# The product of gate and up: runs of seven columns and a strided write, in place of strided reads and a plain write

## The chip, the cores and the metric

The kernel runs on one core of a Trainium2 chip. The metric is device time in microseconds (us) from one execution of the whole kernel; several executions are run, and their median is compared.

A core has five engines with queues of their own: PE (matrix multiply, with weight loads shown as PEld), DVE (VectorE), ACT (ScalarE), POOL (GpSimd) and SP, which here only issues transfers. Sixteen DMA engines move data between the chip's main memory and SBUF, the on-chip memory of 128 partitions. PE writes to PSUM, a second on-chip memory of 128 partitions and eight banks of 512 fp32 columns. Engines wait for each other through semaphores.

## The reference, cut to what matters

One token passes through an attention layer with a long cache and a gated feed-forward layer, both with a layer norm in front and a residual.

```python
x = A_x                                            # (1, 1, 512) bf16
h = x + _A_ref(_layernorm(x), A_k_cache, A_v_cache, A_wq, A_wo)
h2 = h + _B_ref(_layernorm(h), B_w_gate, B_w_up, B_w_down)

def _A_ref(x, k_cache, v_cache, wq, wo):           # 32 query heads, 8 key heads, 65536 keys of 128
    q = x @ wq; scores = q . k * 128 ** -0.5
    return softmax(scores) . v @ wo

def _B_ref(x, w_gate, w_up, w_down):               # 512 -> 1792 -> 512
    g = x @ w_gate; u = x @ w_up
    return (sigmoid(g) * u) @ w_down
```

The caches of keys and values are 128 MiB each, so most of the work is reading 282 MB. What the change touches is `sigmoid(g) * u`, 1792 products.

## The kernel before, in words

There is no planner: every operation is recorded in program order on the queue of one engine by a helper (`op`, and `dma` for transfers), with the names of the operations that it depends on. From these the helper makes the waits. Each queue then runs strictly in that order.

The body walks through eight key heads. SP issues the loads of each head's keys and values in pieces. DVE transposes the keys in 256 blocks (line 531), PE multiplies them with the queries, DVE and ACT make the softmax, and PE multiplies with the values. When the last head is through, PE applies `wo`, and the tail of the kernel follows, one step behind the other:

- `ln_stats` and `ln_rstd` (lines 400 to 414) make the layer norm of `h`; line 834 writes the centred column `hc`.
- Lines 842 to 851: PE multiplies `hc` with the weights of gate, then with those of up. Each result is split over four partitions (0, 32, 64 and 96), 448 columns each, in PSUM banks `GB` and `UB`. Column `14 q + r` of partition `32 c` is element `448 c + 14 q + r` of the 1792, with `q` from 0 to 31 and `r` from 0 to 13.
- Line 854: ACT makes `tanh` of gate; line 855: DVE turns it into the scaled gate `sg2` (fp32, SBUF). Both come before the last matmul of up, which waits for the last weights of up.
- Lines 857 to 863, on DVE, in two halves `i` of seven values of `r` each (`HH`): a product (line 859) multiplies up, read from PSUM, with `sg2`, and writes `hh` (bf16, SBUF) in the order `32 r + q`; a transpose of 32 by 32 blocks (line 863) then turns each block `r` of `hh` into a column of `hhT` with the elements `q` on the partitions. The order on DVE's queue is product 0, transpose 0, product 1, transpose 1. Product 0 waits for the last matmul of up (`gu1`) and for `sg2`; each transpose waits for its product.
- Lines 871 to 882: PE multiplies each of the 14 columns of `hhT` with its rows of `w_down`, in four matmuls a column, so 56 in all. The first waits for transpose 0, the 29th for transpose 1; four loads of `w_down` (`wd0` to `wd3`) are waited for on the way.
- Lines 884 to 886: DVE and ACT copy the sum out of PSUM, and SP stores it.

The instructions run on all 128 partitions, of which four hold values. The tiles: `hh` is 128 by 448 bf16, `hhT` 128 by 480 bf16; the half of a product is 224 elements per partition. The profile writes `sg` for `sg` and `sg2`, and `PS` for all of PSUM.

Some other lines whose rows the prediction uses: 391 and 392 are reductions on DVE over the same 128 by 128 fp32 tile (391 reads every fourth column, 392 the columns in order); 634 is a product that lays out the attention's output; 410 to 412 are layer norm steps on one column; 566 is a reduction of PSUM columns in runs of eight. Line 432 writes four bf16 values per partition, 16 elements apart. Line 500 copies 64 bf16 values per partition on ACT, from runs of 16 to places eight elements apart (`NC` is 8):

```python
dst = bass.AP(tensor=ktw, offset=W0 + NC - 1, ap=[[KTW_ROW, 128], [WJ, 4], [NC, 16]])
src = bass.AP(tensor=qz, offset=64 * h, ap=[[512, 128], [16, 4], [1, 16]])
```

Of the kernel before, what the change touches and what calls it, by code (L numbers as in the profile page):

```python
# [10 lines left out]
ALU = mybir.AluOpType  # L11
# [24 lines left out]
class Prog:  # L36
# [14 lines left out]
    def op(self, eng, fn, deps=(), name=None, to=None, times=1):  # L51
        assert name is None or name not in self.where, name
        self.ops[eng].append(dict(fn=fn, deps=[d for d in deps if d], name=name, dma=None, to=to, times=times, part=self.part.get(eng)))
        if name:
            self.where[name] = (eng, len(self.ops[eng]) - 1)
# [168 lines left out]
def bass_sequential_preLN__gqa_block_cached__glu_gated_glu__decode_kernel(  # L224
# [15 lines left out]
    NF = FF // 128  # L240
# [4 lines left out]
    FG = FF // 4  # L245

    with ExitStack() as es:
        def sb(name, shape, dt):
            return es.enter_context(nc.sbuf_tensor(name, shape, dt))
# [51 lines left out]
        sg2 = sb("sg2", [128, FG], fp32)  # L301
        hh = sb("hh", [128, FG], bf16)
# [12 lines left out]
        def ps(bank, c0, c1, p0=0, p1=128):  # L315
            return PS[p0:p1, bank * 512 + c0: bank * 512 + c1]
# [311 lines left out]
        YT, STB, GB, UB, YB, OT = 0, MISC, 2, 3, 5, (1, 1)  # L628
# [228 lines left out]
        HH = ((0, 7), (7, NF))  # L857
        for i, (r0, r1) in enumerate(HH):
            op("dve", lambda e, r0=r0, r1=r1: e.tensor_tensor(  # L859
                hh[:, 32 * r0:32 * r1].rearrange("p (r q) -> p r q", q=32),  # L860
                ps(UB, 0, FG).rearrange("p (q r) -> p r q", r=NF)[:, r0:r1, :],
                sg2[:, :].rearrange("p (q r) -> p r q", r=NF)[:, r0:r1, :], ALU.mult), ["gu1", "sg2"], f"hh{i}")
            op("dve", lambda e, r0=r0, r1=r1: e.transpose(hhT[:, 32 + 32 * r0:32 + 32 * r1], hh[:, 32 * r0:32 * r1]), [f"hh{i}"], f"hhT{i}")  # L863
        def down(e, out_, lhsT, rhs, g, end):

# [51 lines left out]
```

## Time and profile before

| | |
|---|---|
| runs: median (lowest to highest) | 656.91 us (656.45 to 657.18) |
| span of the profiled execution, first to last instruction | 655.0 us |
| PE busy | 397.5 us (61%) |
| DVE busy | 350.3 us (53%) |
| ACT busy | 43.1 us (7%) |
| moved by DMA | 282.33 MB, mean 431 GB/s |
| mean granted clock of PE | 0.786 |

For the profiled execution the page gives the span alone; against the median of the runs, 1.9 us lie around it.

How to read the rows. A group row has the line, the engine, the operation, what is written and read with its shape and type, the count, and then busy us, mean ns of one | idle us of the engine before them, and what ended it. A timeline row has the start and the length in us ahead of that. A row by stretches has the stretch, its length, then the busy time (and count) of PE, PEld, DVE, ACT and POOL, the granted clock of PE as a share of full speed, the busy share of the DMA engines, and GB/s; where it was asked of one line alone, only that line's engines stand in it. The chain that ended last is followed back from the last instruction: each step is what released the next one. "Issue" is time in which an engine waited for nothing that the profile shows.

### The profile page before, as it was taken

What the parts mean: (1) busy time and instruction counts of PE and PEld (TensorE: products, weight loads), DVE (VectorE), ACT (ScalarE), POOL (GpSimd) and SP (SyncE); (2) the same over time, 40 slices, a digit from 0 to 9 for tenths busy, and PEclk for the clock granted to TensorE, in tenths of its full rate; (3) what the DMA queues carried; (4) which work ended last, traced back from release to release, by engine and by line L of the source; (5) the groups of instructions that cost most, each with busy time, mean ns of one, the idle gap of its engine ahead of it and who ended that gap; (6) DMA issues with size and microseconds to landing.
All of it is one profiled execution on the core that took longest, in us unless ns stands there. A gap on an engine that the chain in (4) does not pass through costs nothing.

```text
span 655.0 us, 6176 instructions
## 1 busy us (share of the span) xinstructions
PE 397.5 (61%) x2317; PEld 66.7 (10%) x1549; DVE 350.3 (53%) x428; ACT 43.1 (7%) x114; POOL 3.7 (1%) x19
## 2 busy tenths in 40 slices
PE   2778672937548293674828467392845739285466
PEld 1100010110101000010100101010010101001122
DVE  3398853819266290935719184481917548092202
ACT  1100200020000200002000200002000020001101
POOL 1000000000000000000000000000000000000000
PEclk9799695977959687785968769596796958878656
DMA  9999999999999999999999999999999989999998
GB/s 400 432 434 462 424 408 448 448 448 412 420 448 448 432 400 448 448 448 404 428 448 448 436 396 448 448 448 416 416 448 448 448 384 448 448 448 424 417 412 363
DMA packets 6372, 282.33 MB, mean 431 GB/s; under 512 B 738, under 2 KB 868, under 8 KB 1252
## 3 DMA queue, kind: packets, MB, share of 16 engines
q1 hardware_dynamic: 6340, 282.33, 99.7%
q10 hardware_dynamic: 32, 0.00, 0.0%
HBM read 282.33 MB, written 0.00 MB: 431 GB/s over the span
## 4 chain that ended last, share of the span: by engine, by line
DMA 66%; DVE 30%; PE 2%; issue 1%; SPq 0%; PEldq 0%
DMA ring<-in_A_k_cache_dram 58%; DVE ktw L531 30%; DMA ring<-in_B_w_up_dram 4%; DMA ring<-in_A_v_cache_dram 4%; PE PS L443 2%; PE PS L866 0%; PE PS L847 0%; DVE hh L859 0%; DVE hhT L863 0%; SPq L368 0%; SPq L339 0%; DVE y_sb L884 0%; PEldq L171 0%
## 5 line engine op out<-in xcount | busy, mean ns | idle before, releaser
L531 DVE STREAM_TRANSPOSE ktw<-ring 128x1024 f32<-128x1024 f32 x256 | 291.5, 1208 | 165.0 <-DMA ring<-in_A_k_cache_dram 165.0
L443 PE MATMUL PS<-ktw 128*128 128x512 bf16 x1024 | 276.3, 419 | 163.4 <-DVE ktw L531 155.8
L443 PE MATMUL PS<-ring,PT_sb 128*32 x1024 | 85.0, 420 | 55.0 <-issue 46.6
L443 PEld LDWEIGHTS PS<-ktw 128*128 x256 | 26.2, 102 | 401.5 <-issue 234.3
L618 ACT ACTIVATE po_sb<-PS,rl 128x512 bf16<-128x512 f32 x8 | 5.5, 687 | 523.4 <-PE PS L443 523.4
L443 PEld LDWEIGHTS PS<-ring,PT_sb 128*32 x1024 | 20.7, 116 | 117.5 <-issue 116.2
L566 DVE TENSOR_REDUCE gmj<-PS 1x4 f32<-1x128 f32 x8 | 2.2, 278 | 53.5 <-PE PS L564 53.5
L538 DVE TENSOR_REDUCE M_sb<-PS 128x1 f32<-128x512 f32 x32 | 19.9, 683 | 19.3 <-PE PS L443 19.3
L577 ACT ACTIVATE P_sb<-PS,negmax 128x512 bf16<-128x512 f32 x32 | 21.6, 686 | 0.3
L587 DVE STREAM_TRANSPOSE PT_sb<-P_sb 128x512 bf16<-128x512 bf16 x32 | 19.9, 674 | 1.7 <-ACT P_sb L577 1.7
L443 PE MATMUL PS<-ktw,xz 128*8 x32 | 9.6, 476 | 6.1 <-DMA ktw<-in_A_wq_dram 6.1
L634 DVE TENSOR_TENSOR Lw<-O,blk_of 128x896 bf16<-128x896 bf16 (+1 forms) x2 | 1.4, 682 | 15.9 <-ACT O L624 15.9
L489 DVE STREAM_TRANSPOSE qt<-qh 32x512 bf16<-32x512 bf16 x1 | 0.7, 699 | 14.8 <-ACT qh L486 14.8
L571 PE MATMUL PS<-one_f,gmrep 1*128 1x1 f32 x16 | 4.7, 358 | 5.0 <-DVE gmrep L568 5.0
L564 PE MATMUL PS<-identf,gm 128*1 128x128 f32 x16 | 4.5, 380 | 5.1 <-issue 2.9
L643 DVE CAST O<-PS 128x28 bf16<-128x28 f32 (+1 forms) x2 | 0.3, 174 | 12.8 <-PE PS L640 12.8
L577 ACT ACTIVATION_READ_ACCUMULATOR P_sb<-PS,negmax 128x1 f32 x32 | 6.5, 203 | 0.0
L621 PE MATMUL PS<-sel_bf,po_sb 128*128 128x4 bf16 x32 | 2.1, 170 | 6.3 <-ACT po_sb L618 6.3
L504 ACT ACTIVATE PS<-zcol 128x512 f32<-128x512 bf16 x8 | 5.0, 622 | 0.0
L573 ACT ACTIVATE negmax<-PS 128x1 f32<-128x1 f32 x8 | 1.4, 171 | 54.0 <-PE PS L571 54.0
L571 PEld LDWEIGHTS PS<-one_f,gmrep 1*128 1x128 f32 x16 | 4.0, 307 | 8.8 <-DVE gmrep L568 8.8
L592 PE MATMUL PS<-L_sb,lsel 128*128 128x4 f32 x16 | 2.5, 229 | 3.8 <-DVE PT_sb L587 3.8
(90 smaller groups left out, 65.4 us busy)
## 6 DMA issues: line engine op xcount, KB each, us to landing
ring<-in_A_k_cache_dram SPq DMA_DIRECT2D x4, 4096.0 KB, 34.8
ring<-in_A_v_cache_dram SPq DMA_DIRECT2D x1, 5120.0 KB, 30.1
ktw<-in_A_wq_dram SPq DMA_DIRECT2D x1, 4096.0 KB, 12.2
ktw<-in_A_wo_dram SPq DMA_DIRECT2D x1, 3584.0 KB, 18.4
ring<-in_A_v_cache_dram SPq DMA_DIRECT2D x1, 3072.0 KB, 36.9
ring<-in_B_w_gate_dram SPq DMA_DIRECT2D x1, 1792.0 KB, 23.4
ring<-in_B_w_up_dram SPq DMA_DIRECT2D x1, 1792.0 KB, 27.2
ring<-in_B_w_down_dram SPq DMA_DIRECT2D x1, 1024.0 KB, 29.2
```

The source lines that it names most:

```text
L443: return e.add_instruction(mybir.InstMatmult(name=nc.get_next_instruction_name(), engine=mybir.EngineType.PE, ins=[rhs, lhsT], outs=[e.low ...
L504: op("act", lambda e: e.activation(ps(PO, 0, 512), bass.AP(tensor=zcol, offset=0, ap=[[1, 128], [0, 512]]), AF.Copy), ["zcol"] if h == 0 e ...
L531: op("dve", lambda e, d=dst, sr=src: e.transpose(d, sr), deps, f"T{b}.{c}", to="T")
L538: op("dve", lambda e, u=u: e.tensor_reduce(M_sb[:, u % 4:u % 4 + 1], ps(u % NS, 0, 512), AX.X, ALU.max), [f"S{b}.{NC - NR + k}"], f"mx{u}" ...
L564: op("pe", lambda e: e.matmul(ps(MISC, 0, 128, 0, 1), lhsT=gm[:, :], rhs=identf[:, :], start=True, stop=True), [f"gm{h}"], f"gmT{h}", to="Q")
L566: op("dve", lambda e: e.tensor_reduce(gmj[:, :], ps(MISC, 0, 128, 0, 1).rearrange("p (i a c) -> p a i c", a=4, c=NC), AX.XY, ALU.max), [f" ...
L571: op("pe", lambda e: e.matmul(ps(MISC, 128, 129), lhsT=gmrep[0:1, :], rhs=one_f[0:1, 0:1], start=True, stop=True), [f"gmrep{h}"], f"neg{h}")
L577: op("act", lambda e, b=b: e.activation(P_sb[:, (b % 4) * 512:(b % 4 + 1) * 512], ps(b % NS, 0, 512), AF.Exp, bias=negmax[:, k:k + 1], sca ...
L587: op("dve", lambda e, b=b: e.transpose(PT_sb[:, (b % 4) * 512:(b % 4 + 1) * 512], P_sb[:, (b % 4) * 512:(b % 4 + 1) * 512]), [f"E{b}"], f" ...
L592: op("pe", lambda e: e.matmul(ps(MISC, 132, 136), lhsT=lsel[:, :], rhs=L_sb[:, :], start=True, stop=True), [f"PT{NR * h + NR - 1}"], f"l{h ...
L618: op("act", lambda e: e.activation(po_sb[:, :], ps(PO, 0, 512), AF.Copy, scale=rl[:, :]), [f"PV{h}.{NR - 1}", f"rl{h}"], f"po{h}", to="po")
L621: op("pe", lambda e, t=t: e.matmul(ps(OX, 0, 4), lhsT=po_sb[:, t * 128:(t + 1) * 128], rhs=sel_bf[:, 8 * t:8 * t + 8:2], start=(t == 0), s ...
```

## The change

Both products of line 859 walk their three operands in another order. Before, the outer loop is over `r` and the inner one over `q`: the reads of up (PSUM) and `sg2` (SBUF) step by 14 fp32 elements, 56 bytes, and the write to `hh` is plain. After, the outer loop is over `q` and the inner one over `r`: the reads go in runs of seven neighbouring fp32 elements, and the write to `hh` steps by 32 bf16 elements, 64 bytes. Each element ends where it did before, and the transposes and all else stay.

```diff
         HH = ((0, 7), (7, NF))
         for i, (r0, r1) in enumerate(HH):
             op("dve", lambda e, r0=r0, r1=r1: e.tensor_tensor(
-                hh[:, 32 * r0:32 * r1].rearrange("p (r q) -> p r q", q=32),
-                ps(UB, 0, FG).rearrange("p (q r) -> p r q", r=NF)[:, r0:r1, :],
-                sg2[:, :].rearrange("p (q r) -> p r q", r=NF)[:, r0:r1, :], ALU.mult), ["gu1", "sg2"], f"hh{i}")
+                hh[:, 32 * r0:32 * r1].rearrange("p (r q) -> p q r", q=32),
+                ps(UB, 0, FG).rearrange("p (q r) -> p q r", r=NF)[:, :, r0:r1],
+                sg2[:, :].rearrange("p (q r) -> p q r", r=NF)[:, :, r0:r1], ALU.mult), ["gu1", "sg2"], f"hh{i}")
             op("dve", lambda e, r0=r0, r1=r1: e.transpose(hhT[:, 32 + 32 * r0:32 + 32 * r1], hh[:, 32 * r0:32 * r1]), [f"hh{i}"], f"hhT{i}")
```

## The prediction

> **What bounds the kernel now.** I read the page first: the span, the line on DMA, and the shares of the chain that ended last.
>
> ```profile
> span 655.0 us, 6176 instructions
> ...
> DMA  9999999999999999999999999999999989999998
> ...
> DMA 66%; DVE 30%; PE 2%; issue 1%; SPq 0%; PEldq 0%
> ```
>
> The 16 DMA engines are busy in every slice: over most of the span the kernel runs at the pace of its loads, with VectorE's transposes next. The change lies in the last five microseconds, so its worth has to be read there. Next came the chain in order of time, cut to its end (start, length, what).
>
> ```profile
> 621.60 27.22 DMA ring<-in_B_w_up_dram
> 648.82 0.04 issue
> 648.86 1.69 PE PS L847 x16
> 650.55 0.02 issue
> 650.58 0.54 DVE hh L859
> 651.12 0.02 issue
> 651.14 0.42 DVE hhT L863
> 651.57 0.14 issue
> 651.70 1.79 PE PS L866 x50
> 653.49 0.03 issue
> 653.51 0.28 DVE y_sb L884
> ```
>
> The last block of weights of up lands at 648.82, its matmuls end at 650.55, and from there every step waits for the one before it. The first product (L859) is on that chain itself. The timeline of the same stretch gives both products, both transposes and the matmuls behind them.
>
> ```profile
> 650.58 0.53 DVE L859 TENSOR_TENSOR hh<-PS,sg 128x224 bf16<-128x224 f32 x1 [1.15 <-PE PS L847]
> 651.14 0.41 DVE L863 STREAM_TRANSPOSE hhT<-hh 128x224 bf16<-128x224 bf16 x1
> 651.48 0.49 DVE L859 TENSOR_TENSOR hh<-PS,sg 128x224 bf16<-128x224 f32 x1
> 651.67 1.43 PEld L866 LDWEIGHTS PS<-ring,hhT 128*32 128x32 bf16 x52 [0.71 <-DMA ring<-in_B_w_down_dram]
> 651.70 1.77 PE L866 MATMUL PS<-ring,hhT 128*32 128x128 bf16 x56 [0.45 <-DVE hhT L863]
> 652.01 0.41 DVE L863 STREAM_TRANSPOSE hhT<-hh 128x224 bf16<-128x224 bf16 x1
> ```
>
> The second transpose ends at 652.01 + 0.41 = 652.42. The table by stretches (PE busy, PEld busy, granted clock, DMA share, GB/s) shows how close behind it the second half of the down projection starts.
>
> ```profile
> 651.70:652.48 0.78, 0.78 (x30) 0.68 (x30) 0.50 1.01 380
> 652.48:653.50 1.02, 0.99 (x36) 0.48 (x24) 0.71 0.18 61
> ```
>
> By 652.48 thirty of the 56 matmuls had started (the 36 of the second row count those still running). The 29th, the first that needs the second transpose, so started about when that transpose ended: there is next to no slack. If the products get longer, the end moves by what both add; if they get shorter, the whole gain cannot come through, since the last weights of down are still landing:
>
> ```profile
> 652.50:653.00 0.50, 0.50 (x27) 0.36 (x24) 0.00 (x0) 0.00 (x0) 0.00 (x0) 0.50 0.32 109
> 653.00:653.50 0.50, 0.47 (x16) 0.17 (x12) 0.00 (x0) 0.00 (x0) 0.00 (x0) 0.93 0.00 0
> ```
>
> DMA moves data until just before 653.0, and the last group of four matmuls needs the last of it.
>
> **The change part by part.** Nothing is added, removed or moved: each engine has the same instructions, in the same order, with the same waits; both instructions of L859 change shape, from 128x224 to 32 by 7. No DMA and no queue is touched. VectorE's queue behind them is as before (transpose, product, transpose, the copy at L884). Three things change in each product: the read of PSUM, the read of the SBUF operand, and the write.
>
> *The reads.* What 224 elements would cost without any stride follows from other products; what a strided read costs, from reductions over the same 128 elements.
>
> ```profile
> L566 DVE TENSOR_REDUCE gmj<-PS 1x4 f32<-1x128 f32 x8 | 2.2, 278 | 53.5 <-PE PS L564 53.5
> ...
> L634 DVE TENSOR_TENSOR Lw<-O,blk_of 128x896 bf16<-128x896 bf16 x1 | 1.1, 1073 | 0.0
> ...
> L391 DVE TENSOR_REDUCE row_of<-identf 128x4 bf16<-128x128 f32 x1 | 0.4, 368 | 0.0
> ...
> L410 DVE TENSOR_TENSOR mo<-mo 128x1 f32<-128x1 f32 x2 | 0.3, 159 | 0.1
> ...
> L634 DVE TENSOR_TENSOR Lw<-O,blk_of 128x128 bf16<-128x128 bf16 x1 | 0.3, 291 | 15.9 <-ACT O L624 15.9
> ...
> L392 DVE TENSOR_REDUCE blk_of<-identf 128x32 bf16<-128x128 f32 x1 | 0.3, 275 | 0.0
> ```
>
> From 128 to 896 elements L634 grows by (1073 - 291) / 768 = 1.02 ns per element, so 224 come to 291 + 96 x 1.02 = 389 ns. L859 takes longer (shortest, middle and longest record of the line):
>
> ```profile
> L859 DVE TENSOR_TENSOR hh<-PS,sg x2: 495/514/532, 650.6 to 651.5; 128x224 bf16<-128x224 f32 x2
> ```
>
> By the timeline the first is the one of 532. So 143 and 106 ns, 0.64 and 0.47 per element, lie above the plain rate. L391 reads in steps of four fp32 and takes 368 where L392, which reads the same tile in order, takes 275: 0.73 ns per strided element. The excess in L859 is therefore the strided read. In runs of seven it should go almost whole (L566 reads PSUM in runs of eight and takes 278 ns for 128 elements, no more than L392). Bounds: nothing gained, or 143 + 106 = 249 ns; I take the full 249.
>
> *The write.* Each bf16 result now goes alone to an address 64 bytes from the last one. No row of VectorE writes many elements this way. The nearest ones:
>
> ```profile
> L412 DVE TENSOR_SCALAR ve<-mo 128x1 f32<-128x1 f32 x2 | 0.3, 155 | 0.1
> ...
> L432 DVE TENSOR_SCALAR xz<-hT,mo,rstd 128x4 bf16<-128x4 f32 x1 | 0.3, 299 | 0.7 <-POOL rstd L414 0.7
> ...
> L500 ACT ACTIVATE ktw<-qz 128x64 bf16<-128x64 bf16 x8 | 3.9, 492 | 0.0
> ...
> L624 ACT ACTIVATE O<-PS 128x4 bf16<-128x4 f32 x8 | 1.4, 174 | 2.8 <-PE PS L621 2.8
> ```
>
> L500, on ScalarE, reads runs of 16 and writes 64 single bf16 values 16 bytes apart: 492 ns, against 174 for the four of L624, which is (492 - 174) / 60 = 5.3 ns per element. L432 writes four bf16 values 32 bytes apart and takes 144 ns longer than L412, at most 36 ns each; but it also reads two scalars per partition, which may be most of that. At the lower end the write hides behind the read at 1.02 ns. Between 1.02 and 36 I take 5.3: the row with the same kind of write, with enough elements to show a rate. It is another engine's row, which is the weak point of this forecast; if the price belongs to the memory it carries over, if to ScalarE it doesn't.
>
> [...]
>
> *The sum.* With one element at 159 ns (L410), a product comes to 159 + 223 x 5.3 = 1341 ns: 809 more than the first, 846 more than the second. The second transpose then ends at 652.42 + 0.81 + 0.85 = 654.08. The first 28 matmuls, 0.8 us long, start 0.81 later at 652.51 and are done by then; PE waits for the second transpose and the remaining 28 run behind it. They took 1.02 us, half of it, up to 653.0, at a granted clock of 0.50; after that it was 0.93. If it is high again by 654, that first 0.5 us could shrink by up to 0.26; I take half, 0.13. The end moves by 0.81 + 0.85 - 0.13 = 1.5 us, the copy and the store behind it unchanged. The transposes keep their 0.41: they read and write the same dense tiles.
>
> The profiled span is 655.0; the median of the runs is 656.91, so 1.9 us lie around the span. Span after: 656.5; time after: 656.91 + 1.5 = **658.4 us**, 0.23% more.
>
> **The rivals.**
> *The write is hidden (the other side).* If VectorE passes one product per cycle and SBUF takes scattered writes at that pace, L859 falls to 389. The first half of down starts 0.14 earlier; the second half cannot use all of the 0.25, because the last weights land just before 653.0. About 0.14 saved: 656.8. It decides if a scattered write costs less than about 1.6 ns ((532 - 159) / 224 = 1.7 and (495 - 159) / 224 = 1.5). For it: L859 itself holds its rate with two strided operands, only 1.4 to 1.6 times slower. Against it: L500.
> [...]
> *The write costs what a strided read costs.* At 1.02 + 0.73 = 1.75 ns, a product is 159 + 223 x 1.75 = 549 ns: +17 and +54, 656.91 + 0.07 = 657.0. [...] Against it: L500 again, three times dearer.
> *The write is dearer than on ScalarE.* At L432's 36 ns a product takes 159 + 223 x 36 = 8.2 us and the end moves by 15.3 at most: 672.2. For it: L432 is VectorE's own. Against: only four elements, and two scalar operands. Values in between (10 ns: 2.39 us a product, +3.75 us, 660.7) belong here too.
> That the change doesn't do what it says I leave out: the instructions have the new shape.
>
> **How the numbers follow.** Scattered write near 5.3 ns: 0.52, own range 657.9 to 659.2 (4.4 to 6.5 ns). Like a strided read: 0.22. Hidden: 0.12. Dearer: 0.14. About 0.2%, 1.3 us, is what a measurement of this kernel can tell from no change; the likeliest case lies close above it, so 0.08 of its 0.52 falls inside. Slower by more: 0.44 + 0.14 = 0.58. Within: 0.08 + 0.22 + 0.10 = 0.40. Faster by more: 0.02, which no case here gives by its own sum, left to the hidden one for the spread of the runs. Range: down to 656.6, a little below the hidden case; up to 661.5, which takes in write prices to about 12 ns and leaves 0.08 of the dearer case out.
>
> **What would show it.** The two records of L859: 1.34 us each if I am right, 0.39 if the write is hidden, 0.55 if it costs as a read does, several us if dearer. A second idle stretch on PE of about 0.7 us between the two halves of L866, put down to the second transpose; none in the two rivals near no change. The transposes at 0.41 and everything before 650.5 unchanged; if L863 grows instead, the writes outlive the product's own record. The prediction is wrong if ScalarE's price is ScalarE's own, or if the write price depends on the distance (16 bytes in L500, 64 here).

## The result

The changed kernel takes 658.28 us (median of ten runs, 657.21 to 658.86) against 656.66 us (656.45 to 657.18) before: ratio 1.0022, 95% interval 1.0014 to 1.0030. It is slower, by 1.6 us between the medians, and the profiled execution has a span of 656.2 us in place of 655.0. The 656.91 us from which the prediction counts was the median of three runs of the kernel before; with ten it is 656.66.

### The profile page after: what moved, and what is told of

The parts are those of the page before. It is cut to its first block, busy times and chain, and to the rows that moved or that the text cites. A ratio compares the mean times of both kernels' runs of the same rounds, so it can differ in the third digit from the quotient of the medians.

```text
span 656.2 us, 6176 instructions
## 1 busy us (share of the span) xinstructions
PE 398.6 (61%) x2317; PEld 66.8 (10%) x1549; DVE 351.6 (54%) x428; ACT 43.1 (7%) x114; POOL 3.7 (1%) x19
## 4 chain that ended last, share of the span: by engine, by line
DMA 66%; DVE 30%; PE 3%; issue 1%; SPq 0%; PEldq 0%
DMA ring<-in_A_k_cache_dram 58%; DVE ktw L531 29%; DMA ring<-in_B_w_up_dram 4%; DMA ring<-in_A_v_cache_dram 4%; PE PS L443 2%; DVE hh L859 0%; PE PS L847 0%; PE PS L866 0%; DVE hhT L863 0%; SPq L368 0%; SPq L339 0%; DVE y_sb L884 0%; PEldq L171 0%
## 5 line engine op out<-in xcount | busy, mean ns | idle before, releaser
L443 PE MATMUL PS<-ring,PT_sb 128*32 x1024 | 86.6, 427 | 54.0 <-issue 45.5
```

What stands on the lines that cost most here:

```text
L443: return e.add_instruction(mybir.InstMatmult(name=nc.get_next_instruction_name(), engine=mybir.EngineType.PE, ins=[rhs, lhsT], outs=[e.low ...
```

## The profile after

The timeline of the changed kernel's tail (start and length in us, then the row) answers to the one shown before:

```profile
650.65 1.13 DVE L859 TENSOR_TENSOR hh<-PS,sg 128x224 bf16<-128x224 f32 x1 [0.91 <-PE PS L847]
651.82 0.41 DVE L863 STREAM_TRANSPOSE hhT<-hh 128x224 bf16<-128x224 bf16 x1
652.15 1.11 DVE L859 TENSOR_TENSOR hh<-PS,sg 128x224 bf16<-128x224 f32 x1
...
652.38 0.94 PE L866 MATMUL PS<-ring,hhT 128*32 128x128 bf16 x28 [1.05 <-DVE hhT L863]
653.30 0.41 DVE L863 STREAM_TRANSPOSE hhT<-hh 128x224 bf16<-128x224 bf16 x1
...
653.77 0.94 PE L866 MATMUL PS<-ring,hhT 128*32 128x128 bf16 x28 [0.45 <-DVE hhT L863]
```

The two products have grown from 0.53 and 0.49 us to 1.13 and 1.11. The 56 matmuls of down, one block before, have fallen into two of 28 with PE idle between them until the second transpose. The chain that ended last now runs through both products:

```profile
650.65 1.14 DVE hh L859
651.79 0.02 issue
651.82 0.41 DVE hhT L863
652.23 1.05 DVE hh L859
653.27 0.02 issue
653.30 0.42 DVE hhT L863
653.72 0.04 issue
653.77 0.96 PE PS L866 x24
654.73 0.02 issue
654.75 0.28 DVE y_sb L884
```

From the start of the first product to the copy at L884 (called the stretch below) it is 654.75 - 650.65 = 4.10 us; before it was 653.51 - 650.58 = 2.93. The profile so shows 1.17 us more in the tail. All records of L859, to the nanosecond:

```profile
L859 DVE TENSOR_TENSOR hh<-PS,sg x2: 1112/1120/1128, 650.7 to 652.2; 128x224 bf16<-128x224 f32 x2
```

Against 495 and 532 that is 0.62 + 0.60 = 1.21 us, so the products account for the whole of it.

## The experiments

**Read or write.** Two kernels do one half of the change each. The first keeps the reads in runs of seven and writes plainly:

```diff
-                hh[:, 32 * r0:32 * r1].rearrange("p (r q) -> p q r", q=32),
+                hh[:, 32 * r0:32 * r1].rearrange("p (q r) -> p q r", q=32),
```

> The products read in runs of seven as in the changed kernel, and write plainly (hh then holds the elements in the order 7 q + r, so the output is of another order of the products: this run is for time alone). Theory W (the price is that of the scattered bf16 write): both records of L859 near 0.39 us, the stretch from the start of the first product to the start of the copy at L884 near 2.8 us (before 2.93, changed 4.10), time within 0.1% of before. Rival R (the price is that of reading 32 short runs of seven): L859 near 1.1 us, the stretch near 4.1, time +1.2 us or more.

The second reads plainly and keeps the strided write:

```diff
-                ps(UB, 0, FG).rearrange("p (q r) -> p q r", r=NF)[:, :, r0:r1],
-                sg2[:, :].rearrange("p (q r) -> p q r", r=NF)[:, :, r0:r1], ALU.mult), ["gu1", "sg2"], f"hh{i}")
+                ps(UB, 32 * r0, 32 * r1).rearrange("p (q r) -> p q r", q=32),
+                sg2[:, 32 * r0:32 * r1].rearrange("p (q r) -> p q r", q=32), ALU.mult), ["gu1", "sg2"], f"hh{i}")
```

> The products read 224 neighbouring elements and write with the 64-byte step of the changed kernel (other products meet, so this run is for time alone). Theory W: L859 near 1.12 us each, the stretch from the first product to the copy near 4.1 us, +1.2 us against before. Rival R: L859 near 0.39 us, the stretch near 2.8 us, no change in time.

The first took 656.66 us, ratio 1.0000 (0.9990 to 1.0009); the second 658.00, ratio 1.0021 (1.0012 to 1.0030). Their timelines, the first kernel's ahead:

```profile
651.00 0.39 DVE L859 TENSOR_TENSOR hh<-PS,sg 128x224 bf16<-128x224 f32 x1 [0.92 <-PE PS L847]
...
651.76 0.35 DVE L859 TENSOR_TENSOR hh<-PS,sg 128x224 bf16<-128x224 f32 x1
...
653.93 0.28 DVE L884 CAST y_sb<-PS 33x128 bf16<-33x128 f32 x1 [1.38 <-PE PS L866]
```

```profile
651.11 1.13 DVE L859 TENSOR_TENSOR hh<-PS,sg 128x224 bf16<-128x224 f32 x1 [0.96 <-PE PS L847]
...
652.61 1.11 DVE L859 TENSOR_TENSOR hh<-PS,sg 128x224 bf16<-128x224 f32 x1
...
655.21 0.28 DVE L884 CAST y_sb<-PS 33x128 bf16<-33x128 f32 x1 [1.04 <-PE PS L866]
```

The price is that of the write alone: with it the product has the length that it has in the changed kernel (1.13 and 1.11 us), without it 0.39 and 0.35. The runs of seven cost nothing (0.39 us in the price list below, with 0.38 for the plain product).

The stretch of the first kernel is 653.93 - 651.00 = 2.93 us, no shorter than before, although its products are 0.28 us shorter in sum. Its chain that ended last says why:

```profile
623.00 30.33 DMA ring<-in_B_w_down_dram
653.33 0.04 issue
653.37 0.29 PE PS L866 x6
```

It no longer passes through VectorE: the last weights of down land at 653.33, and the rest follows from there, the copy 0.60 us later.

**A price list.** The kernel before, with further products of 224 elements put into VectorE's idle time at the start, and copies on ScalarE; two of the 17 products as a sample:

```diff
+        def tt(dims, n, t=None, src=None, sps=None):
+            return lambda e: e.tensor_tensor(bass.AP(tensor=t or P_sb, offset=0, ap=[[512 if t else 2048, 128]] + dims), psap(5, 0, sps or n),
+                                             bass.AP(tensor=ms, offset=0, ap=[[448, 128]] + (src or n)), ALU.mult)
+        op("dve", tt([[1, 8], [8, 28]], [[28, 8], [1, 28]]), ["mv2"], "mv3")
+        op("dve", tt([[2, 16], [32, 7], [1, 2]], [[14, 16], [2, 7], [1, 2]]), ["mv8"], "mv9")
```

> The kernel before, with 17 further products of 224 elements (PSUM times SBUF) on VectorE and seven copies on ScalarE, put into the idle time of both at the start, into tiles not yet in use. Writes at steps of 4, 8, 16, 32, 64 and 128 bytes in bf16, of 32 and 64 bytes in fp32, in runs of 2, 4 and 8 bf16 values 64 bytes apart; then four read patterns with a plain write. Theory W, one price per touched 16-byte line: plain 0.39 us; from 16 bytes on 1.12 us whatever the distance; at 4 and 8 bytes a half to a quarter of the excess; runs of two 0.55 to 0.65, of four and eight near 0.39; fp32 like bf16 if the price is of the line, 0.39 to 0.55 if it is of the two-byte value. If the distance itself counts (banks), 64 bytes is dearer than 16. Strided reads 0.50 to 0.53, runs of seven 0.39 to 0.42. On ScalarE the 64 single values 0.49 us, plain 64 near 0.24; if the price is the memory's, 224 single values take 0.9 us or more above plain there too.

The table by stretches, cut to the line of these products, one stretch for each (start:end, length, then VectorE's busy time; the last three columns are PE's clock and the load on DMA). In order: plain, then bf16 at steps of 4, 8, 16, 32, 64 and 128 bytes; fp32 at 32 and 64 bytes; pairs of bf16 64 bytes apart (runs of four and eight gave the same 0.39). After the first gap, with a plain write: PSUM read in steps of 56 bytes, SBUF read so, and both in runs of seven.

```profile
8.64:9.05 0.41, 0.38 (x1) 1.00 0.55 240
9.05:9.49 0.44, 0.41 (x1) 1.00 2.24 968
9.49:10.18 0.69, 0.65 (x1) 1.00 0.00 0
10.18:11.36 1.18, 1.15 (x1) 1.00 1.03 444
11.36:12.51 1.15, 1.12 (x1) 1.00 1.06 456
12.51:13.67 1.16, 1.13 (x1) 1.00 1.05 452
13.67:14.86 1.19, 1.16 (x1) 1.00 1.02 441
14.86:15.46 0.60, 0.56 (x1) 1.00 1.64 710
15.46:16.03 0.57, 0.53 (x1) 1.00 0.40 172
16.03:16.46 0.43, 0.39 (x1) 1.00 1.41 610
...
17.31:17.73 0.42, 0.39 (x1) 1.00 1.99 858
17.73:18.30 0.57, 0.53 (x1) 1.00 0.67 287
...
18.87:19.29 0.42, 0.39 (x1) 1.00 1.44 624
```

With one element at 0.16 us (L410), single bf16 writes come to (1.13 - 0.16) / 223 = 4.3 ns each at 64 bytes, 4.4 at 16, 4.3 at 32 and 4.5 at 128: from 16 to 128 bytes the distance hardly matters. At 8 bytes it is half of that, (0.65 - 0.16) / 223 = 2.2, and at 4 bytes 1.1, hardly above the plain product. One price of 4.4 ns for each 16 bytes touched would give just these; what in the memory these 16 bytes would be, no run shows. But it holds only for single two-byte values: fp32 values 32 and 64 bytes apart cost 1.7 to 1.8 ns each (a plain fp32 write is not in the list), and pairs of bf16 nothing (0.39 us), though they touch half as many places, 64 bytes apart, as the single ones do. So single two-byte values pay the price (4.3 to 4.5 ns), and four neighbouring bytes, as a pair or as one fp32 value, do not, or far less. Two bytes alone do not make it dear, though: at steps of 4 bytes each value stands alone too, and four of them come to one price (4 x 1.1 ns). Why is not shown. Pairs that start at an odd place were not run; they would tell whether the place of the four bytes counts or any two neighbours in a row do.

Of the reads, only the SBUF operand pays for the step of 56 bytes (0.53, as in the kernel before); PSUM read in the same steps takes the plain 0.39, where 0.50 to 0.53 had been expected.

ScalarE's copies in the same way: 64 bf16 values plainly and at a step of 16 bytes, then 224 plainly and at steps of 16 and 64 bytes:

```profile
3.39:3.66 0.27, 0.24 (x1) 1.00 0.29 122
3.66:4.17 0.51, 0.48 (x1) 1.00 0.16 64
...
4.69:5.11 0.42, 0.39 (x1) 1.00 0.00 0
5.11:6.34 1.23, 1.20 (x1) 1.00 0.99 426
6.34:7.54 1.20, 1.17 (x1) 1.00 1.01 437
```

From 64 to 224 single values it is (1.20 - 0.48) / 160 = 4.5 ns each. Two engines have the same price within a few per cent, 4.3 and 4.5 ns. This points to the memory's side of the write, but does not show it.

**Pairs in the changed kernel.** The order of the change, with two neighbouring `q` innermost, so that each write is a pair:

```diff
-                hh[:, 32 * r0:32 * r1].rearrange("p (r q) -> p q r", q=32),
-                ps(UB, 0, FG).rearrange("p (q r) -> p q r", r=NF)[:, :, r0:r1],
-                sg2[:, :].rearrange("p (q r) -> p q r", r=NF)[:, :, r0:r1], ALU.mult), ["gu1", "sg2"], f"hh{i}")
+                hh[:, 32 * r0:32 * r1].rearrange("p (r h t) -> p h r t", h=16, t=2),
+                ps(UB, 0, FG).rearrange("p (h t r) -> p h r t", t=2, r=NF)[:, :, r0:r1, :],
+                sg2[:, :].rearrange("p (h t r) -> p h r t", t=2, r=NF)[:, :, r0:r1, :], ALU.mult), ["gu1", "sg2"], f"hh{i}")
```

> The order of the changed kernel, but with two neighbouring values of q innermost: each write is a pair of bf16 values (4 bytes) 64 bytes from the last one, and the reads step by 56 bytes again within a pair. Theory V (a single two-byte value has to be merged into its word, a whole word has not): L859 0.39 to 0.55 us, the stretch from the first product to the copy about 2.95 us, time as before. Rival L (a price per 16-byte line that is touched, with 4.4 ns for each): 112 lines, 0.65 us or more, the stretch 3.2 us.

```profile
650.57 0.39 DVE L859 TENSOR_TENSOR hh<-PS,sg 128x224 bf16<-128x224 f32 x1 [1.12 <-PE PS L847]
...
651.34 0.35 DVE L859 TENSOR_TENSOR hh<-PS,sg 128x224 bf16<-128x224 f32 x1
...
652.95 0.14 PEld L866 LDWEIGHTS PS<-ring,hhT 128*32 128x32 bf16 x8 [0.30 <-DMA ring<-in_B_w_down_dram]
...
653.55 0.28 DVE L884 CAST y_sb<-PS 33x128 bf16<-33x128 f32 x1 [1.42 <-PE PS L866]
```

The products take 0.39 and 0.35, the time is that of before: 656.55 us, ratio 1.0000 (0.9990 to 1.0009). The whole loss of the change hangs on writing single two-byte values (1.13 and 1.11 us). That a single value is merged into its word, as theory V has it, these times do not show. The reads, which jump by 56 bytes and back with each pair, cost nothing here either, `sg2` in SBUF included: 393 and 352 ns, where the kernel with runs of seven and a plain write has 392 and 352. The stretch is 653.55 - 650.57 = 2.98 us: again no gain, and again PE waits for the last weights of down, until 652.95, with the copy 0.60 us behind.

**Could it be faster than before?** The one strided read that costs was moved off the chain: L855 writes the gate in the order in which the product needs it.

```diff
-        op("dve", lambda e: e.tensor_scalar(sg2[:, :], sg[:, :], 1.0, rstd[1][:, 0:1], op0=ALU.add, op1=ALU.mult), ["sg"], "sg2")
+        op("dve", lambda e: e.tensor_scalar(sg2[:, :].rearrange("p (r q) -> p r q", q=32), sg[:, :].rearrange("p (q r) -> p r q", r=NF), 1.0, rstd[1][:, 0:1], op0=ALU.add, op1=ALU.mult), ["sg"], "sg2")
-                sg2[:, :].rearrange("p (q r) -> p r q", r=NF)[:, r0:r1, :], ALU.mult), ["gu1", "sg2"], f"hh{i}")
+                sg2[:, 32 * r0:32 * r1].rearrange("p (r q) -> p r q", q=32), ALU.mult), ["gu1", "sg2"], f"hh{i}")
```

> The kernel before, with the scaled gate written in the order r, q by L855 (which then reads with the step of 56 bytes), so that the product reads SBUF and writes plainly and only its read of PSUM keeps the step of 56 bytes. From the price list: L859 0.39 us each, L855 0.7 to 0.8 in place of 0.45, hidden ahead of the last matmul of up. The stretch from the first product to the copy: 2.8 us if VectorE sets the end (the prediction's rival of a hidden write), 2.93 as before if the last weights of down set it, which land 2.3 us after the first product starts. Time within 0.1% of before in both.

L855 took 0.61 us, less than expected and hidden; the products 0.39 and 0.35. The time did not move: 656.58 us, ratio 1.0004 (0.9994 to 1.0013), the stretch 653.70 - 650.66 = 3.04 us. PE waited for the last weights of down, which landed at 653.09:

```profile
653.13 0.52 PE L866 MATMUL PS<-ring,hhT 128*32 128x128 bf16 x12 [0.28 <-DMA ring<-in_B_w_down_dram]
```

No version of this product found here beats the kernel before; at best it ties. The kernel before stands at that limit already: in a run below whose products are as before (the hidden scattered product), the chain that ended last comes from these weights too, landing at 652.90, with the copy at 653.50.

**Do the two products add up?** The first alone was changed:

```diff
-            op("dve", lambda e, r0=r0, r1=r1: e.tensor_tensor(
+            op("dve", (lambda e, r0=r0, r1=r1: e.tensor_tensor(
+                hh[:, 32 * r0:32 * r1].rearrange("p (r q) -> p q r", q=32),
+                ps(UB, 0, FG).rearrange("p (q r) -> p q r", r=NF)[:, :, r0:r1],
+                sg2[:, :].rearrange("p (q r) -> p q r", r=NF)[:, :, r0:r1], ALU.mult)) if i == 0 else lambda e, r0=r0, r1=r1: e.tensor_tensor(
```

> The first product alone as in the changed kernel, the second as before. Theory W (the two records add up on the way to the second transpose, with no slack behind it): L859 1.13 and 0.50 us, the stretch from the first product to the copy at L884 3.5 us (before 2.93, changed 4.10), half of the change's loss. Rival S (the second half of the matmuls has slack, so that one late product is hidden or the second alone counts): the stretch stays below 3.1 us.

```profile
650.49 1.13 DVE L859 TENSOR_TENSOR hh<-PS,sg 128x224 bf16<-128x224 f32 x1 [1.14 <-PE PS L847]
...
651.99 0.49 DVE L862 TENSOR_TENSOR hh<-PS,sg 128x224 bf16<-128x224 f32 x1
...
653.96 0.28 DVE L887 CAST y_sb<-PS 33x128 bf16<-33x128 f32 x1 [1.03 <-PE PS L869]
```

The stretch is 653.96 - 650.49 = 3.47 us, 0.54 of the 0.60 added; the second product adds the remaining 0.63. The time: 657.28, ratio 1.0010 (1.0000 to 1.0019). They add up, nearly without slack.

**Is it all in the tail?** Run again, the changed kernel lost 1.3 us between the medians, with 1.17 in its tail by the profile.

> The changed kernel again. The two products account for +0.60 and +0.62 us, and the tail of the chain for +1.17 in the profile (4.10 against 2.93 us). If the whole difference lies there, the medians differ by 1.2 us (ratio 1.0018); if there is more (the medians so far differ by 1.6), it stays at 1.0025 and something outside the tail has become longer as well.

657.83 us against 656.53, ratio 1.0021 (1.0012 to 1.0030). The spans of single executions show a second part: in the 27 runs of before the span has a median of 655.2 us and the whole lies 1.37 us above it on average; in the changed kernel's first ten runs 656.2 and 1.92, in these eleven 656.2 and 1.76. So 1.0 us is in the span, and some 0.4 to 0.5 us on average around it, from runs (ten of 21) with 2.0 to 2.6 us there in place of 1.3. Three kernels ask whether scattered writes do that. Two delay the tail with a plain product into another tile in front of each product, 448 and 528 elements long (the second, not printed, takes its 528 from two passes over 264 elements of `sg2`):

```diff
+            op("dve", lambda e, i=i: e.tensor_tensor(P_sb[:, 512 * i:512 * i + FG], sg2[:, :], sg2[:, :], ALU.mult), ["gu1", "sg2"])
```

> The kernel before, with a plain fp32 product of 448 elements into an unused tile in front of each of the two products: 0.61 us each, so that the chain grows by about 1.2 us without any scattered write. If only the length of the tail counts: the time grows as that of the changed kernel does (ratio near 1.002), and the time between the span and the whole, 1.3 us in nearly all runs of before and up to 2.6 in half of those of the changed kernel, spreads the same way. If the scattered writes themselves do something past their record: ratio 1.0018 and 1.3 us around the span throughout.

> The delay without scattered writes, 528 plain elements in place of 448 in front of each product, so that the stretch from its first product to the copy is that of the changed kernel, 4.1 us. If the end of the chain alone makes the loss: span as in the changed kernel, 656.2 to 656.4, ratio 1.0017 to 1.0022. If the changed kernel loses something besides: ratio below 1.0020 with 1.3 to 1.6 us around the span in every run, and the remainder, some 0.3 us on average, belongs to the time around the span.

The third puts a scattered product where it is hidden:

```diff
+        op("dve", lambda e: e.tensor_tensor(bass.AP(tensor=P_sb, offset=0, ap=[[2048, 128], [1, 28], [32, 7]]),
+                                            bass.AP(tensor=sg2, offset=0, ap=[[FG, 128], [7, 28], [1, 7]]),
+                                            bass.AP(tensor=sg2, offset=0, ap=[[FG, 128], [7, 28], [1, 7]]), ALU.mult), ["sg2"])
```

> The kernel before, with one product of 196 scattered bf16 writes (64 bytes apart, into a tile no longer used) put between L855 and the wait for the matmuls of up: about 1.0 us, in a gap of 1.15 us. If only the way to the end counts: the product is hidden, the stretch from the first product of L859 to the copy stays at 2.93 us, ratio 1.000, and about 1.3 us lie between span and whole. If scattered writes, or the program that holds them, cost something outside the span: some runs show 2.0 us and more there, as 13 of the 31 runs of the kernels with the change's write did, against 1 of 60 of before.

The shorter delay grew the stretch by 1.0 us and not by the expected 1.2, to 654.43 - 650.49 = 3.94, since each product starts before the record of the delay ends (651.03 against 651.11, 652.43 against 652.50). It gave 657.79, ratio 1.0016 (1.0007 to 1.0025), span 656.2, with 1.3 to 1.6 us around the span in all eleven runs. The longer one (stretch 654.82 - 650.69 = 4.13) gave 658.02, ratio 1.0022 (1.0013 to 1.0031), span 656.4, and five of eleven runs with 2.0 to 2.4 us around it: the changed kernel's loss and its spread, without a scattered write. The hidden scattered product (1.01 us for 196 writes) cost nothing: 656.48, ratio 1.0001 (0.9992 to 1.0010), stretch 2.93, and one run of eleven with more than 2 us. So the spread does not need the writes. With a stretch of 4.1 us it shows in 18 of 42 runs, in the kernel before in 2 of 81. But the later end alone is not shown to bring it on either: the shorter delay has the changed kernel's span and none of it, and the kernel with `sg2` in another order, which ends no later than before, has two runs of ten with 2.8 us.

The traces hold a lead. The pages of three of the four kernels with a stretch of 4.1 us have a row that no other page has:

```profile
q8 instruction: 1, 0.02, 0.0%
```

It is one packet of 16 KB on a queue that the profile marks as instruction. In the repeat of the changed kernel, the longer delay and the kernel with plain reads and the strided write it starts before the last instruction ends (at 656.1, 656.1 and 655.4), and these executions have 1.3 us around the span. In the first profile of the changed kernel it starts at 657.5, 1.3 us after the end of the span and so past what the page covers, and 2.2 us lie around that span. The other traces have no such packet at their end, but for the price list, with two of 8 KB after its span and 3.5 us around it. A late load of instructions would so explain the long runs. With one trace a kernel it is not shown, and what calls for the load stays open.

## Why the prediction was right, and where it was off

- *The stretch and its slack: right.* Both products lie on the chain, next to no slack behind them: 0.54 us of the first one's 0.60 came through, and all of the second one's 0.62 (0.63).
- *The reads: about right in size, wrong in place.* 143 and 106 ns were taken as gained; with a plain write the records of L859 are 392 and 352 ns, 140 and 143 shorter than before. (The second is the shorter one in every version, so 389 was too high a plain time for it.) But the sentence on the strided read put the excess down to the strided reads as such, and PSUM has no part in it (0.39 us with PSUM read in steps of 56 bytes, 0.53 with SBUF read so).
- *The write: right row, 5.3 ns where 4.3 was measured.* The row of ScalarE was the right neighbour: the price carried over. The term was mis-sized where the rest of L500 was taken from the four values of L624, 174 ns: between 64 and 224 single values the same engine gives 4.5, which leaves 492 - 64 x 4.5 = 204 ns for the rest. The sum had 1.66 us for both products and they cost 1.21; 4.3 lies just under the 4.4 at which the forecast's own range begins. The worry that 64 bytes might be dearer than 16 was void (4.3 and 4.4 ns). L432's 36 ns, the dearer rival, was not the write: it is ruled out by the price list.
- *The clock: off, small.* 0.13 us was taken off for a clock recovered by 654. It was not:

```profile
653.77:654.75 0.98, 0.93 (x28) 0.67 (x28) 0.00 (x1) 0.00 (x1) 0.00 (x0) 0.50 0.00 0
```

The granted clock stays at 0.50 through the second half of the matmuls; they took 0.98 us all the same, where 1.02 had been counted less 0.13.
- *Around the span: a term that was missing.* The sum kept 1.9 us there for both kernels. That figure is the median of three runs less one profiled span; over 27 runs of before it is 1.37 on average, and with the change 0.4 to 0.5 more. This and the write's price nearly cancel: 1.66 us less 0.13 were forecast, and 1.0 to 1.2 in the span with 0.4 to 0.5 around it were found. That the 1.5 us forecast come so close to the 1.3 to 1.6 measured is in part luck.
- *The hidden rival* would have saved 0.14 us, it was said. Its place is shown by three kernels with products at 0.39 and 0.35: they save nothing, for the last weights of down set the end. The bound was named, but sized 0.14 us too far off. One product per cycle was the author's supposition: the runs show these times, no cycle.

## What to carry to other kernels

Single two-byte values, written 16 to 128 bytes apart, cost 4.3 to 4.5 ns each here, more than four times the plain product's 1.0 ns per element ((0.38 - 0.16) / 223); written in pairs 64 bytes apart they cost nothing above it (0.39 us for 224, against 0.38). When one side of a product has to be strided, let it be the read of PSUM, then that of SBUF, and the bf16 write last (0.39, 0.53 and 1.13 us for 224 elements here). And look at what lands next before shortening a chain: here a transfer stood right behind it, and a faster product could only tie.

## What was not expected of the hardware

PSUM read in steps of 56 bytes at the plain rate (0.39 us for 224 elements, against 0.53 for SBUF). Pairs of bf16 written 64 bytes apart at the plain rate too, against 4.3 ns for each single one. And the time around the span, which rose from 1.3 to 2.0 us and more in 18 of 42 runs once the tail was 1.2 us longer, with scattered writes or without.
